# Window attention and a SiLU MLP: products nobody reads, and each pair's work queued one and two pairs later

## The chip, the cores and the metric

The kernel runs on one core of a Trainium2 chip. The core has a matrix engine (TensorE, PE in the profile; its weight loads are PEld), a vector engine (VectorE, DVE), a scalar engine (ScalarE, ACT), GpSimd (POOL), and a queue that issues its transfers (SP). Each engine takes its instructions strictly in the order of its own queue and waits where an input isn't there yet or a buffer isn't free; TensorE's weight loads overlap its products. TensorE writes to PSUM, eight banks of 512 fp32 columns on 128 partitions. The metric is device time in microseconds; lower is better.

## The reference

Eight batches of eight heads, 576 positions, head size 64, all fp32. Attention looks back over 128 positions with a slope on the distance; its output, heads side by side, is the input of an MLP with SiLU:

```python
scores = scale * np.matmul(q, k.transpose(0, 1, 3, 2))
...
mask = (rel >= 0) & (rel < window)          # window = 128
scores = np.where(mask, scores + bias[None], -1000000000.0)
scores = scores - np.max(scores, axis=-1, keepdims=True)
attn = np.exp(scores)
attn = attn / (np.sum(attn, axis=-1, keepdims=True) + 1e-09)
...
h = x @ w_in                                # 4608 x 512 @ 512 x 2048
g = h * (1.0 / (1.0 + np.exp(-h)))
return (g @ w_out).astype(np.float32)       # 4608 x 2048 @ 2048 x 512
```

## The kernel before

The 4608 rows are 36 tiles of 128, made into 9 groups of 512 rows (4 tiles). Attention is done in 72 pairs, two for each tile (a pair is one tile and four of the eight heads). The MLP goes group by group: for each of 16 blocks f of 128 hidden columns, `gemm1` (L379) makes h, `act1` to `act4` make SiLU of it split in a high and a low part, and `gemm2` (L412) adds it to four output tiles. All operands are split in high and low parts, so that three fast products stand for one of full precision. The weights arrive as raw bits and are split on the chip in 32 pieces (`w_split1` on ScalarE, `w_shift` and `w_low` on VectorE, `w_hi` on ScalarE, `w_lo` on VectorE, L448 to L476); four pieces, the list `W_EARLY`, are split ahead of the MLP, the other 28 during its first group.

A pair p goes through these steps; the letters are used from here on. **S(p)** (`scores`, L205): q times k, 16 products (8 in the first tile of a pair of batches, which has no tile behind it). **R(p)** (`row_max`, L229): VectorE adds the slope table and takes the row's maximum, into one of three buffers `t`. **E(p)** (`exps`, L240): ScalarE's exponentials. Then, for the first eight pairs, **T(p)** (`p_transpose_first`, L268), 8 transposes on TensorE into the two PSUM banks "h"; **H(p)** (`p_hi_first`, L278), ScalarE's high part; and **L(p)** (`p_lo_first`, L284), VectorE's low part. **A(p)** (`attend`, L291): 24 small products with v (12 in the first tile), into one of two PSUM banks with the tag "a", of which it uses 260 columns. **N(p)** (`normalize`, L311): VectorE divides by the sum and writes x. Later pairs transpose by DMA instead.

v is scaled by a power of two that comes from its maximum over a pair of batches: nine loads (`vscale_load`, L120), nine reductions (`vscale_reduce`, L127), and three last steps with two small products vt and vs (`vscale_finish`, L141); for the first batches all of that lies at the start of the kernel. GpSimd and VectorE then split v (`v_hi`, `v_lo`, L183 to L199). The scale loads of later batches and the plain v loads share two buffers, "rv".

The order of the work is written out by hand. `put(point, function, ...)` (L481) files a call under a point in time, `at(p)` (L60) gives the point at which pair p begins, and at each point what was filed is issued in the order of filing, each instruction to its engine's queue. Points below zero are the **opening**: pairs 0 to 7, 8 points apart (`STEP`), whose x is then transposed on TensorE (`x_transpose`, L350, PSUM banks "a"), copied to `xh` by ScalarE and `xl` by VectorE. From point 0 on each half of a `gemm1` or `gemm2` is one point, so a group has 64, and the later pairs lie between them. In the opening S(p) stands at n = at(p), R at n+1 and n+2, E at n+2 and n+3, T at n+3 and n+4, H at n+4 and n+5, L at n+11 and n+12, A at n+14, N at n+15 and n+16. So TensorE's queue holds S(p+1), T(p+1), A(p), S(p+2), and so on.

Of the kernel before, what the change touches and what calls it, by code (L numbers as in the profile page):

```python
# [6 lines left out]
F32 = mybir.dt.float32  # L7
F32R = mybir.dt.float32r
F16 = mybir.dt.float16
BF16 = mybir.dt.bfloat16  # L10
# [6 lines left out]
P = 128  # L17
B, H, S, D = 8, 8, 576, 64
NHP = H // 2
DM, DFF = 512, 2048  # L20
# [11 lines left out]
GT = TG // P  # L32
# [17 lines left out]
STEP = 8  # L50
# [3 lines left out]
WD = (1, 1, 2, 3)  # L54

CLOSE = (-4, 2, 8, 14, 20, 26, 32, 38)
W_EARLY = (-18, -15, -9, -6)


def at(p):  # L60

    if p < 2 * GT:
        return STEP * (p - 2 * GT) - 14
    if p < 4 * GT:
        return CLOSE[p - 2 * GT]
    return STEP * (p - 2 * GT) - LEAD
# [3 lines left out]
def tile_window_attention_then_silu_mlp(ctx, tc, qk, v, w_in, w_out, base8, out):  # L70
    nc = tc.nc

    const = ctx.enter_context(tc.tile_pool(name="const", bufs=1))
    pool = ctx.enter_context(tc.tile_pool(name="pool", bufs=2))
    psum = ctx.enter_context(tc.tile_pool(name="psum", bufs=1, space=PSUM))

    ident = const.tile([P, P], F32, name="ident")
    tab = const.tile([P, H, 2 * P], BF16, name="tab")
    ones = const.tile([P, P], F32, name="ones")
    v1 = const.tile([P, VSLOTS, H, D + 1], F16, name="v1")  # L80
    v2 = const.tile([P, VSLOTS, H, D], F16, name="v2")
    weights = {}
# [26 lines left out]
    def next_tag(use):  # L109
        turn[use] = turn.get(use, -1) + 1  # L110
        return bank[use][turn[use] % len(bank[use])]

    def ps_of(tag, name):
        return psum.tile([P, DM], F32, tag=tag, bufs=2 if tag in "ah" else 1, name=name)


    vsc = {}
# [2 lines left out]
    def vscale_load(b, i):  # L120

        tag, bufs = (LAST[XD + i], 1) if b == 0 else ("rv", 2)
        t = pool.tile([P, DM], F32, tag=tag, bufs=bufs, name=f"vm{b}_{i}")
        nc.sync.dma_start(t, v[b, i * P : (i + 1) * P, :])
        vred.setdefault(b, {})[i] = t
# [41 lines left out]
    def block_of(i):  # L167
        return i % NBLK

    def load_k(i):  # L170
        ks[i] = pool.tile([P, NHP, P], F32, tag="k", bufs=KSLOTS, name=f"k{i}")
        nc.sync.dma_start(ks[i], qk[i, 1])

    def load_q(i):
        qs[i] = pool.tile([P, NHP, P], F32, tag="q", bufs=2, name=f"q{i}")
        nc.sync.dma_start(qs[i], qk[i, 0])
# [173 lines left out]
    def x_transpose(cc):  # L350
        xp = ps_of(next_tag("misc"), f"xp{cc}")
        for i in range(GT):
            nc.tensor.transpose(xp[:, i * P : (i + 1) * P], xt[i][:, cc * P : (cc + 1) * P], ident)
        nc.scalar.copy(xh[:, cc], xp)  # L354
        nc.vector.tensor_sub(xl[:, cc], xp, f32(xh[:, cc]))  # L355
# [7 lines left out]
    def x_send():  # L363

        if not w_done():
            return
        for i in [i for i in whole if i // GT <= now[0] + 1]:
            whole.remove(i)
            x_dma(i)

    def x_parts(i):
        t, first = xt[i & -2, "t"][:, i % 2], i % GT * P
        cols, scale = slice(first, first + P), vsc[i // NBLK][:, 1:2]
        nc.scalar.activation(xh[:, :, cols], t[:, :NCC], AF.Copy, scale=scale)  # L374
        nc.gpsimd.tensor_scalar(xl[:, :, cols], t[:, NCC:], scale, 1.0, op0=ALU.mult, op1=ALU.mult)  # L375
# [16 lines left out]
    def act1(n):  # L392
        gt = pool.tile([P, TG], F32, tag="gt", name=f"gt{n}")
        nc.scalar.activation(gt, hps[n], AF.Tanh, scale=0.5 / W_SCALE)  # L394
        gact[n] = gt
# [85 lines left out]
    def put(point, fn, *a):  # L481
        plan.setdefault(max(point, at(0)), []).append((fn, a))

    for p in range(NPAIR):
        i, q = divmod(p, 2)
        n = at(p)
        a = n + (14 if p < 2 * GT else 15 if p < 4 * GT else 13)
        put(n, scores, p)
        if block_of(i) in (SPLIT, SPLIT + 1):
            put(n + 1, other_batch, p)  # L490
        put(n + 1, row_max, p, 0)
        put(n + 2, row_max, p, 1)
        put(n + 2, exps, p, 0)
        put(n + 3, exps, p, 1)
        if p < 2 * GT:
            put(n + 3, p_transpose_first, p, 0)
            put(n + 4, p_hi_first, p, 0)
            put(n + 4, p_transpose_first, p, 1)
            put(n + 5, p_hi_first, p, 1)
            put(n + STEP + 3, p_lo_first, p, 0)  # L500
            put(n + STEP + 4, p_lo_first, p, 1)
        else:
            put(n + 3, p_hi, p, 0)
            put(n + 4, p_lo, p, 0)
            put(n + 4, p_hi, p, 1)
            put(n + 4, p_transpose, p, 0)
            put(n + 5, p_lo, p, 1)
            put(n + 5, p_transpose, p, 1)
        put(a + 0, attend, p)
        put(a + 1, normalize, p, 0)  # L510
        put(a + 2, normalize, p, 1)
        put(a + 3, x_hi, p)
        put(a + 3, x_lo, p)
        if q == 0:
            if i > 1:
                put(at(2 * i - 3) + 1, load_q, i)
                put(at(2 * i - 3) + 1, load_k, i)
            if i >= GT:
                put(n - 2, load_v, i)
            put(a - 3, v_hi, i)  # L520
            put(a - 2, v_lo, i)
    for b in range(1, NBB):
        n = at(2 * NBLK * b)
        for i in range(VCH):
            put(n - 10 * STEP + i * STEP, vscale_load, b, i)
            put(n - 10 * STEP + i * STEP + 6, vscale_reduce, b, i)
        for x in range(3):
            put(n - 6 + 2 * x, vscale_finish, b, x)

# [2 lines left out]
    def later(n, fn, *a):  # L532
        put(pos[0] + n, fn, *a)
# [25 lines left out]
    def begin():  # L559
        for fn, a in plan.pop(pos[0], []):  # L560
            fn(*a)

    with tc.manual_schedule():
        make_identity(nc, ident)
        nc.gpsimd.memset(ones, 1.0)

        warm = const.tile([P, 1], F32, name="warm")
        nc.scalar.activation(warm, ones[:, :1], AF.Exp)
        load_q(0)
        load_k(0)  # L570
        nc.sync.dma_start(tab[:, :, P:], base8[:, :, P:])
        for i in range(VCH):
            vscale_load(0, i)
        load_q(1)
        load_k(1)
        nc.sync.dma_start(tab[:, :, :P], base8[:, :, :P])
        nc.gpsimd.memset(v1[:, :, :, D : D + 1], 1.0)
        for i in range(VCH):
            put(at(0) + 3 + i // 2, vscale_reduce, 0, i)
        for x in range(3):  # L580
            put(at(0) + 8 + x, vscale_finish, 0, x)
        for n in range(2):
            put(at(0) + 14 + 8 * n, w_next_load)
        for n in W_EARLY:
            put(n, w_next)
        for cc, n in enumerate((17, 18)):
            put(at(2 * GT - 2) + n, x_transpose, cc)
        while pos[0] < 0:
            begin()
            pos[0] += 1  # L590
        bank.update(scores=[("a", "a")])

        for g in range(NG):
            now[0] = g

            seq = []
            for f in range(NF):
                n = g * NF + f
                seq += [("g1", n, 0)] + [("xt", 0, 2), ("xt", 0, 3)] * (n == 0) + [("g1", n, 1)]
                if 0 < f < NF - 1:  # L600
                    seq += [("g2", n - 1, 0), ("g2", n - 1, 1)]
            n = g * NF + NF - 1
            for i, x in enumerate([("g2", n - 1, 0), ("g2", n - 1, 1), ("g2", n, 0), ("g2", n, 1)]):
                if g + 1 < NG:
                    seq.append(("xt", g + 1, i))
                seq.append(x)
            for k, n, half in seq:
                if k == "xt":
                    if n == 0:
                        x_transpose(half)  # L610
                    else:
                        x_parts(n * GT + half)
                    continue
                begin()
                x_send()
                if k == "g1":
                    gemm1(n, half)
                    if half == 1:
                        act1(n)
                        later(1, act2, n)  # L620
                        later(2, act3, n)
                        later(2, act4, n)
                else:
                    gemm2(n, half)
                    if n % NF == NF - 1:
                        store(g, 2 * half)
                        store(g, 2 * half + 1)
                if g == 0 and half == 0:
                    w_next()
                pos[0] += 1  # L630
        while plan:
            begin()
            pos[0] += 1
# [35 lines left out]
```

## Time and profile before

| | |
|---|---|
| time, median of 3 runs | 1061.81 us (1060.4 to 1065.43) |
| the profiled execution | 1063.14 us, its span 1061.4 us |
| busy TensorE, VectorE, ScalarE, GpSimd | 996.7, 554.4, 463.4, 248.5 us |
| first S | 4.73 us |
| last S of the opening, S(7) | 55.13 us |
| first product of the MLP | 71.64 us |

The page shows one execution: the busy time of each engine, the span in 40 slices (a digit is the busy share in tenths; PEclk is TensorE's granted clock in tenths of full speed), and the costliest groups of instructions. The timeline gives for each entry start, length, engine, line, operation, what it writes and reads, and in brackets how long the engine stood idle before it and what ended that. A stretch by engine has its length, the busy time of each engine with instructions in brackets, the granted clock, the DMA engines' busy share and GB/s. A busy TensorE is not one at full speed.

### The profile page before, as it was taken

To read this page: it belongs to the slowest core of one execution; us is meant where nothing else is said; L and a number is where in the kernel's file an instruction comes from. 1 tells how busy PE (TensorE), PEld (TensorE's weight loads), DVE (VectorE), ACT (ScalarE), POOL (GpSimd) and SP (SyncE) were. 2 spreads that over 40 slices of the span, in tenths; PEclk is the share of its full clock that TensorE was granted. 3 is DMA by queue.
4 is the path that set the end of the run, shared out by engine and by line. 5 is a ranking of instruction groups with operands and counts; after the bars stand their busy time and mean duration, and the time that the engine had idled before them with its cause. 6 is when DMAs were issued, how large, how long until landed. Compare 5 with 4: busy or idle time off the path is not lost. (4 is left out here: it accounts for less than half of the span.)

```text
span 1061.4 us, 16664 instructions
## 1 busy us (share of the span) xinstructions
PE 996.7 (94%) x6260; PEld 788.0 (74%) x6260; DVE 554.4 (52%) x1358; ACT 463.4 (44%) x968; POOL 248.5 (23%) x228
## 2 busy tenths in 40 slices
PE   4669999999999999999999999999999999999998
PEld 3557777677767776777677777777677777787886
DVE  3568899555546554545455554555455545542111
ACT  4356667534344445434444444433433343333222
POOL 3002222322222222222322222222222222223221
PEclk9968999999999999999999999999899999999999
DMA  6147787623454443433354445433334333331001
GB/s 208 41 138 203 190 234 228 150 60 80 80 126 103 100 100 90 110 70 76 74 110 100 99 100 116 102 69 82 90 80 80 81 100 81 61 48 50 1 1 40
DMA packets 201071, 104.89 MB, mean 99 GB/s; under 512 B 168224, under 2 KB 176416, under 8 KB 200992
## 3 DMA queue, kind: packets, MB, share of 16 engines
q1 hardware_dynamic: 200992, 103.84, 41.4%
q8 instruction: 49, 0.80, 0.3%
q14 instruction: 30, 0.25, 0.1%
HBM read 54.00 MB, written 9.44 MB: 60 GB/s over the span
## 5 line engine op out<-in xcount | busy, mean ns | idle before, releaser
L410 POOL TENSOR_TENSOR gl<-gt,gh 128x512 fp32r<-128x512 f32 x144 | 187.2, 1300 | 749.4 <-ACT gh L405 588.1
L394 ACT ACTIVATE gt<-h 128x512 f32<-128x512 f32 x144 | 86.1, 598 | 453.2 <-PE h L387 445.9
L422 PE MATMUL o<-woh,gh 128*128 128x512 f32 x576 | 232.1, 403 | 12.4 <-ACT gh L405 12.4
L387 PE MATMUL h<-xh,wih 128*128 128x512 f32 x576 | 240.3, 417 | 3.3 <-ACT xh L354 3.3
L399 DVE SCALAR_TENSOR_TENSOR gt<-gt,h 128x512 f32<-128x512 f32 x144 | 98.9, 687 | 266.0 <-ACT gt L394 266.0
L422 PE MATMUL o<-woh,gl 128*128 128x512 f32 x576 | 232.1, 403 | 5.4 <-POOL gl L410 5.3
L422 PE MATMUL o<-wol,gh 128*128 128x512 f32 x576 | 229.3, 398 | 0.0
L387 PE MATMUL h<-xh,wil 128*128 128x512 f32 x576 | 228.3, 396 | 0.0
L387 PE MATMUL h<-xl,wih 128*128 128x512 f32 x576 | 227.9, 396 | 0.0
L258 DVE SCALAR_TENSOR_TENSOR hr<-t,hr 128x512 f16<-128x512 f32 (+1 forms) x128 | 120.6, 942 | 80.0 <-ACT hr L253 79.5
L422 PEld LDWEIGHTS o<-woh,gh 128*128 128x128 f32 x576 | 109.5, 190 | 39.5 <-ACT gh L405 15.5
L422 PEld LDWEIGHTS o<-woh,gl 128*128 128x128 f32 x576 | 109.6, 190 | 36.6 <-POOL gl L410 10.6
L387 PEld LDWEIGHTS h<-xh,wih 128*128 128x128 f32 x576 | 109.4, 190 | 31.5 <-ACT xh L354 3.6
L244 ACT ACTIVATE t<-t,mx 128x256 f32<-128x256 f32 (+1 forms) x288 | 120.5, 486 | 26.8 <-DVE mx L234 26.8
L422 PEld LDWEIGHTS o<-wol,gh 128*128 128x128 f32 x576 | 109.7, 190 | 25.7
L387 PEld LDWEIGHTS h<-xh,wil 128*128 128x128 f32 x576 | 109.1, 189 | 25.5
L387 PEld LDWEIGHTS h<-xl,wih 128*128 128x128 f32 x576 | 109.7, 191 | 20.6 <-DVE xl L355 0.4
L234 DVE CUSTOM_DVE_ANT_0 t<-sp,tab 128x256 f32<-128x256 f32 (+1 forms) x288 | 101.0, 404 | 19.9 <-PE sp L214 13.6
L405 ACT CAST gh<-gt 128x512 fp32r<-128x512 f32 x144 | 88.5, 614 | 48.3 <-DVE gt L399 45.9
L344 DVE TENSOR_TENSOR x<-xs,x 128x256 f16<-128x256 f32 x64 | 73.2, 1143 | 44.7 <-ACT x L338 44.7
L214 PEld LDWEIGHTS sp<-k,q 64*128 64x128 f32 x1088 | 74.2, 205 | 29.6 <-issue 23.8
L214 PE MATMUL sp<-k,q 64*128 64x128 f32 x1088 | 89.2, 306 | 5.3 <-DMA k<-qk 4.7
(62 smaller groups left out, 648.6 us busy)
## 6 DMA issues: line engine op xcount, KB each, us to landing
q<-qk SPq DMA_DIRECT2D x36, 256.0 KB, 3.1
k<-qk SPq DMA_DIRECT2D x36, 256.0 KB, 3.2
vm<-v SPq DMA_DIRECT2D x36, 256.0 KB, 3.6
out<-ot SPq DMA_DIRECT2D x36, 256.0 KB, 2.1
wr<-w_in SPq DMA_DIRECT2D x16, 512.0 KB, 3.9
wr<-w_out SPq DMA_DIRECT2D x16, 512.0 KB, 4.1
rv<-v SPq DMA_DIRECT2D x32, 256.0 KB, 2.9
hl<-hr SPq DMA_TRANSPOSE x128, 3.1
```

The lines of the kernel that those rows point to most:

```text
L214: nc.tensor.matmul(sp[h][:, u, o], qs[i][rows, 2 * q + u], ks[i - 1 + o][rows, 2 * q + u], start=True, stop=True, skip_group_check=True,)
L234: nc.vector.tensor_tensor_reduce(out=t[:, h, 2 * P - n :], in0=st[p]["sp"][h][:, u, o].rearrange("p o c -> p (o c)"), in1=tab[:, 4 * q + 2 ...
L244: nc.scalar.activation(x, x, AF.Exp, bias=st[p]["mx"][:, 2 * u + h : 2 * u + h + 1], scale=-1.0)
L258: nc.vector.scalar_tensor_tensor(out=hr[:, 1], in0=t[:, :, 2 * P - n :], scalar=PSCALE, in1=hr[:, 0], op0=ALU.mult, op1=ALU.subtract)
L344: nc.vector.tensor_sub(xt[i][:, 1, cols], st[p]["x"], xt[i][:, 0, cols])
L387: nc.tensor.matmul(hps[n], w[:, cc], x, start=(half == 0 and i == 0), stop=(half == 1 and i == len(seq) - 1), skip_group_check=True,)
L394: nc.scalar.activation(gt, hps[n], AF.Tanh, scale=0.5 / W_SCALE)
L399: nc.vector.scalar_tensor_tensor(out=gt, in0=gt, scalar=1.0, in1=hps[n], op0=ALU.add, op1=ALU.mult)
L405: nc.scalar.copy(gh, gt)
L410: nc.gpsimd.tensor_sub(gl, gt, f32(gh))
L422: nc.tensor.matmul(ops[ti], a[:, t], w, start=(f == 0 and i == 0), stop=(f == NF - 1 and i == len(seq) - 1), skip_group_check=True,)
```

## The change

For the eight pairs of the opening, T(p) and H(p) move from n+3 .. n+5 to n+9, which is just behind S(p+1) and, on ScalarE, ahead of E(p+1). A(p) moves from n+14 to n+18, behind S(p+2) and T(p+1), and N(p) to n+21 and n+22. L(p) stays at n+11 and n+12. The opening begins 4 points earlier, and the points of the early weight pieces and of the two first `x_transpose` are set anew.

`keep_warm(n)` adds n products of two bf16 tiles full of ones (128 rows, 128 by 252 columns) into columns that A doesn't use of the last allocated bank "a"; nobody reads them. 16 stand ahead of all else, 26 between S(0) and S(1), and for each of the eight pairs 4 behind T(p) and 5 ahead of A(p), 114 in all. They need the tile of ones, for which GpSimd has one more memset; the other memset of ones now comes ahead of the identity.

For the later batches the nine scale loads stand 5 points apart instead of 8, from 54 points ahead of the first use of that scale instead of 80, and each is reduced 4 points after its load instead of 6. For later pairs the expression for N's point is written in another way with the same value.

```diff
-W_EARLY = (-18, -15, -9, -6)
+W_EARLY = (-21, -17, -12, -8)
...
     if p < 2 * GT:
-        return STEP * (p - 2 * GT) - 14
+        return STEP * (p - 2 * GT) - 18
...
+    ones16 = const.tile([P, 2 * P], BF16, name="ones16")
...
+    spare = {}
+
     def ps_of(tag, name):
-        return psum.tile([P, DM], F32, tag=tag, bufs=2 if tag in "ah" else 1, name=name)
+        t = psum.tile([P, DM], F32, tag=tag, bufs=2 if tag in "ah" else 1, name=name)
+        if tag == "a":
+            spare["a"] = t
+        return t
+
+    def keep_warm(n):
+
+        for _ in range(n):
+            nc.tensor.matmul(
+                spare["a"][:, 4 * (D + 1) :], ones16[:, :P], ones16[:, : DM - 4 * (D + 1)],
+                start=True, stop=True, skip_group_check=True,
+            )
...
-        a = n + (14 if p < 2 * GT else 15 if p < 4 * GT else 13)
+        a = n + (2 * STEP + 2 if p < 2 * GT else 15 if p < 4 * GT else 13)
...
         if p < 2 * GT:
-            put(n + 3, p_transpose_first, p, 0)
-            put(n + 4, p_hi_first, p, 0)
-            put(n + 4, p_transpose_first, p, 1)
-            put(n + 5, p_hi_first, p, 1)
+
+            put(n + STEP + 1, p_transpose_first, p, 0)
+            put(n + STEP + 1, p_hi_first, p, 0)
+            put(n + STEP + 1, p_transpose_first, p, 1)
+            put(n + STEP + 1, p_hi_first, p, 1)
             put(n + STEP + 3, p_lo_first, p, 0)
             put(n + STEP + 4, p_lo_first, p, 1)
+
+            put(n + STEP + 1, keep_warm, 4)
+            put(n + 2 * STEP + 2, keep_warm, 5)
...
         put(a + 0, attend, p)
-        put(a + 1, normalize, p, 0)
-        put(a + 2, normalize, p, 1)
-        put(a + 3, x_hi, p)
-        put(a + 3, x_lo, p)
+        z = a + (3 if p < 2 * GT else 1)
+        put(z, normalize, p, 0)
+        put(z + 1, normalize, p, 1)
+        put(z + 2, x_hi, p)
+        put(z + 2, x_lo, p)
...
         for i in range(VCH):
-            put(n - 10 * STEP + i * STEP, vscale_load, b, i)
-            put(n - 10 * STEP + i * STEP + 6, vscale_reduce, b, i)
+            put(n - 54 + 5 * i, vscale_load, b, i)
+            put(n - 50 + 5 * i, vscale_reduce, b, i)
...
     with tc.manual_schedule():
+        nc.gpsimd.memset(ones16, 1.0)
+        nc.gpsimd.memset(ones, 1.0)
         make_identity(nc, ident)
-        nc.gpsimd.memset(ones, 1.0)
+        ps_of("a", "warm")
+        keep_warm(16)
...
+        put(at(0) + 4, keep_warm, 10)
+        put(at(0) + 6, keep_warm, 10)
+        put(at(0) + 7, keep_warm, 6)
         for n in W_EARLY:
             put(n, w_next)
-        for cc, n in enumerate((17, 18)):
+        for cc, n in enumerate((23, 24)):
             put(at(2 * GT - 2) + n, x_transpose, cc)
```

## The prediction

> **What bounds the kernel now.** I read the page's slices first, then the opening (the attention of pairs 0 to 7, ahead of the first MLP product) in the timeline, then busy time by stage. S, R, E, T, H, L, A, N are the steps of a pair as the kernel section names them.
>
> ```profile
> PE   4669999999999999999999999999999999999998
> PEclk9968999999999999999999999999899999999999
> 130.00:150.00 20.00, 18.18 (x120) 14.01 (x118) 19.56 (x43) 14.78 (x32) 6.48 (x4) 1.00 0.84 229
> ```
>
> TensorE (PE) is full in 36 of 40 slices; only the first three, some 80 us, are poor. The third line is a stage of the first token group (columns: length, busy PE, weight loads, VectorE, ScalarE, GpSimd, clock, DMA share, GB/s): VectorE is busy 19.56 of 20 us there, because it splits the weights. So that group is VectorE's, later ones are TensorE's, and neither has an anchor in absolute time: what the opening saves shifts all the rest. This is one step of the opening, from S(4) to S(5):
>
> ```profile
> 33.91 2.08 PE L214 MATMUL sp<-k,q 64*128 64x128 f32 x16
> 36.02 0.42 DVE L234 CUSTOM_DVE_ANT_0 t<-sp,tab 128x256 f32<-128x256 f32 x1 [1.11 <-PE sp L214]
> 36.55 1.71 ACT L244 ACTIVATE t<-t,mx 128x256 f32<-128x256 f32 x4 [3.25 <-DVE mx L234]
> 37.41 1.28 DVE L287 SCALAR_TENSOR_TENSOR hl<-pt,hl 128x512 f16<-128x512 f32 x2
> 38.24 1.94 PE L276 MATMUL pt<-ident,t 128*128 128x128 f32 x8 [2.25 <-DVE hl L287]
> 39.36 0.60 ACT L282 ACTIVATE hl<-pt 128x512 f16<-128x512 f32 x1 [1.10 <-PE pt L276]
> 39.97 1.52 PE L304 MATMUL av<-v,hl 128*128 128x65 f16 x24
> 41.42 2.07 PE L214 MATMUL sp<-k,q 64*128 64x128 f32 x16
> 41.53 0.22 DVE L317 TENSOR_SCALAR r<-av,vsc 128x4 f32<-128x4 f32 x1 [2.84 <-PE av L304]
> 42.00 0.42 DVE L328 TENSOR_TENSOR x<-av,r 128x256 f32<-128x256 f32 x1
> ```
>
> S(4), R(4), E(4), T(4) form a chain, with A(3) queued behind T(4). A step lasts 7.51 us (33.91 to 41.42), and TensorE stands idle for 2.25 of it, until R, L(3) and E are done.
>
> The products are also slow. The same S and A later in the kernel (the chain of waits: start, length, what), and the clock in stretches of 1 us (columns as above):
>
> ```profile
> 874.84 0.74 PE av L304 x24
> 877.07 2.79 PE o L422 x12
> 879.86 1.09 PE sp L214 x16
> ...
> 45.71 0.42 PEld L276 LDWEIGHTS pt<-ident,t 128*128 128x128 f32 x4 [2.51 <-ACT t L244]
> 45.74 1.29 PE L276 MATMUL pt<-ident,t 128*128 128x128 f32 x8 [2.25 <-DVE hl L287]
> ...
> 46.50:47.50 1.00, 1.00 (x16) 0.97 (x16) 0.00 (x0) 0.94 (x2) 0.00 (x0) 0.64 0.08 18
> 49.50:50.50 1.00, 0.83 (x8) 0.56 (x6) 0.13 (x1) 0.00 (x0) 0.00 (x0) 0.66 0.00 0
> 53.50:54.50 1.00, 1.00 (x18) 0.95 (x17) 0.00 (x0) 0.92 (x2) 0.00 (x0) 0.55 0.00 0
> 56.50:57.50 1.00, 0.67 (x8) 0.41 (x4) 0.29 (x1) 0.00 (x0) 0.00 (x0) 0.74 0.00 0
> ```
>
> S takes 2.08 here and 1.09 at 880, A 1.52 and 0.74: the opening runs at half clock. (The clock column's 1.00 before about 46 us is no measurement; S at 33.91 is slow all the same.) If each of the four mixed stretches has one change between 0.5 and 1.0, the changes lie at 46.78 (down), 50.18 (up), 53.6 (down) and 57.02 (up): every 3.4 us a decision. The window 46.78 to 50.18, which A and S fill, is followed by full clock; the next, with an idle 2.25, by half. One window back from this grid, 33.1 to 36.5 was filled to 36.0 (S at 33.91 and an A before it), some 85%, and T at 38.24 was still slow. So a nearly full window is needed, and the present order hardly ever gives one.
>
> **The change, part by part.** *The order.* T(p) and H(p) go behind S(p+1), and A(p) behind S(p+2). In a step k the queues then hold: PE S(k), T(k-1), nine dummies, A(k-2); VectorE R(k), L(k-1), N(k-2); ScalarE H(k-1), E(k). Each wants results from a step earlier. ScalarE has 2 x 0.60 + 1.71 = 2.9 us per step; VectorE R 1.39 (36.02 to 37.41), L 1.28 and N 0.89 (41.53 to 42.42), 3.56 together. Three t buffers suffice: the second half of R(k) waits for half of T(k-1), which is through at 1.6 us into the step, before R's first half ends at 1.8.
>
> *The dummies.* No row shows a bf16 product of 252 columns. At full clock A's product of 65 columns takes 0.74/24 = 31 ns and the MLP's of 512 takes 2.79/12 = 233 ns; the dummy lies between, by columns 252/512 x 233 = 115 ns. Nine cost 0.28 to 2.1, I take 1.03, and at half clock 2.06. They are only a gain through the clock: they fill the windows.
>
> *The step.* T at full clock: weight loads of 0.42 for four, so 0.84 for eight; PE's row of 1.29 has a pause in it; I take 1.0. Step = 1.09 + 1.0 + 1.03 + 0.74 = **3.86 us**, above VectorE's 3.56 and ScalarE's 2.9, and without an idle window. At half clock: 2.08 + 1.73 (38.24 to 39.97) + 2.06 + 1.45 (39.97 to 41.42) = 7.32.
>
> *The start.* All nine v tiles must have come before their scale is known, and A(0) waits for v that GpSimd splits by it:
>
> ```profile
> 15.66 0.56 PE L159 MATMUL vs<-vcol,ones 1*128 1x2 f32 x2 [1.16 <-DVE vcol L156]
> 19.13 0.76 PE L304 MATMUL av<-v,hl 128*128 128x64 f16 x11 [1.10 <-POOL v L194]
> 19.82 2.08 PE L214 MATMUL sp<-k,q 64*128 64x128 f32 x16
> ```
>
> Nothing in the change touches this; the 42 early dummies lie in TensorE's wait for these loads and cost nothing unless they run past vt (some 14.1; at half clock by up to 0.6). S(2) now waits for vs alone, not for A(0): 16.22 instead of 19.82. Half clock: S(2) to 18.30, T(1), four products, to 19.2, nine dummies to 21.2, A(0), twelve products, to 21.9. That is a filled window, so S(3) changes to full clock on its way: with 1.6 + 1.0 + 1.03 + 0.37 S(4) stands at 25.9, and three steps on **S(7) at 37.5**, against 55.13 below. If the clock comes two steps later: 44.4; if the early dummies' clock is kept: 35.5.
>
> *The tail.* From S(7) to the second half of the first MLP product:
>
> ```profile
> 55.13 2.04 PE L214 MATMUL sp<-k,q 64*128 64x128 f32 x16
> 60.58 0.66 ACT L451 ACTIVATE wm<-wr 128x512 f32<-128x512 f32 x1
> 61.27 0.43 DVE L457 TENSOR_SCALAR wm<-wm 128x512 int32<-128x512 int32 x1 [1.40 <-ACT wm L451]
> 61.73 0.69 DVE L462 SCALAR_TENSOR_TENSOR wm<-wr,wm 128x512 int32<-128x512 int32 x1
> 62.46 0.62 ACT L472 CAST wih<-wm 128x512 fp32r<-128x512 f32 x1 [0.73 <-DVE wm L462]
> 63.11 0.69 DVE L476 TENSOR_TENSOR wil<-wm,wih 128x512 fp32r<-128x512 f32 x1 [0.34 <-ACT wih L472]
> 64.19 1.33 PE L353 MATMUL xp<-ident,x 128*128 128x128 f32 x5 [1.45 <-DVE x L328]
> 65.32 0.69 DVE L355 TENSOR_TENSOR xl<-xp,xh 128x512 fp32r<-128x512 f32 x1
> 66.06 0.27 PE L304 MATMUL av<-v,hl 128*128 128x65 f16 x2 [0.55 <-DVE xl L355]
> 69.63 2.08 PE L214 MATMUL sp<-k,q 64*128 64x128 f32 x16
> 71.64 0.79 PE L387 MATMUL h<-xh,wih 128*128 128x512 f32 x1
> 72.53 0.79 DVE L225 MEMSET sp<- 64x384 f32 x2
> 76.82 0.61 ACT L139 ACTIVATE vm<-vm 128x512 f32<-128x512 f32 x1
> 78.59 0.80 PE L387 MATMUL h<-xh,wih 128*128 128x512 f32 x1 [3.31 <-ACT xh L354]
> ```
>
> Before: 23.46 us (55.13 to 78.59). After, counted from S(7): H(6) and E(7) end at 4.65 (1.09 for S, 0.6 for half of T, 1.25 and 1.71); the first weight piece's split, shift, low and hi (now ahead of H(7) in ScalarE's queue) end at 7.15; H(7) 8.4; the second piece's split, shift and low 10.25; L(7), behind them on VectorE, 11.55; its last part and N(6) 13.15; then xp and xh up to xl 14.3 (as 64.19 to 65.32), xl 15.0, third piece's shift and low 16.1, second xl 16.8. The five dummies ahead of A(7) write into the xp tile that this xl reads, so they wait for it, where A(7) waited only for the first xl (66.06): 1.8 us later, and 1.15 for the dummies at half clock, since TensorE idled. A(7) 18.0, S(8) 19.4, first MLP product 21.4. Then the stretch of 6.06 from the MEMSET to 78.59 loses two pieces of work already done or moved (a last part of 0.69, a v tile's |max| of 0.61), leaving 4.8 to 5.2: **26.4**. The tail is thus 2.9 us worse, 0 to 6 at the bounds (no wait of the dummies; one more piece ahead of A(7)).
>
> *The loads of v for the second batch pair's scale* come at 12, 17, ... 52 instead of -14, -6, ... 50: the same nine loads and |max|, two of which left the opening, reduced 4 positions after the load instead of 6. They share two buffers with the other v loads, and SP's queue stands still where neither is free (before and after at point 18, until 21). A position of the first group is some 1.9 us; a load that lands later than 7.6 us would hold up ScalarE. I take 0, bounds -1 and +4. GpSimd's memsets at the start swap places and get one more, all under the wait for the first loads: nothing.
>
> *Sum.* 78.59 - (37.5 + 26.4) = 14.7 us. The profiled run took 1063.14 (span 1061.4), 1.3 above the median of 1061.81: 1048.4 against the former, 1047.1 against the latter, forecast **1048**. Bounds: opening 35.5 to 44.4, tail 23.5 to 29.5, v loads -1 to +4, which rarely add up: 1041 to 1057.
>
> **The rivals.** *Half clock throughout*, the slower one: TensorE's clock unit doesn't take transposes, or products of ones, for work. Then steps cost 7.32: S(4) at 28.5, S(7) at 50.5; S, T and A in the tail add 2.9 to 26.4, 79.8 in all, 1.2 later than now, and the late early dummies 0.5: **1065**, 1070 if the dummies' weight loads aren't hidden. It decides once four of the five steps are slow (4 x 3.46 is what I forecast to gain). For it: no window with transposes in it was full in the trace. Against: windows of A and S were enough, and dummies, A and S make 5.6 us on end. 8%.
>
> Beside it a rule: the Trainium skill ("TensorE: Matmul & The Clock Gate", Part 4: PE-mode transpose) says that transposes don't count as activity in the same way, so that full clock doesn't engage for them. The eight at 45.74 did run at full clock, but whether they earn it no row here shows.
>
> *Clock half of the time*, as transposes counted for nothing would make it: 1.0 of each 3.86 empty, full clock won on dummies, A and S and lost again in some windows. Three steps at (3.86 + 7.32)/2 add 5.2, and the tail 1.5: **1055**. 10%.
>
> *VectorE takes TensorE's place:* if S, R, L and N followed on each other, a step were 1.09 + 1.39 + 1.28 + 0.89 = 4.65, 0.8 more in four steps: **1051**, inside my range; for it speaks 3.56 of 3.86, against it that L and N wait on no S of their step. 10%.
>
> *The opening isn't what starts the MLP:* ScalarE's and VectorE's weight splits, in the tail's order, or the loads of v hold it, and only 2 to 5 us arrive: **1058**. For it: the tail already is their chain. Against: all four pieces are loaded before. 7%.
>
> **How the numbers follow.** The forecast has 65%. A measurement of this kernel tells 0.5% (5.3 us) from no change. Faster (under 1056.5): 65, VectorE's 10, 6 of the clock's 10 and 2 of the last 7, 83%; same: 4 + 4 and 3 of the slow rival's 8, 11%; slower: the other 5 and 1, 6%. The range 1041 to 1058 leaves out the slow rival, part of the last one, and a little on the fast side.
>
> **What would show it.** Right: S(2) near 16.2, S about 1.1 and A 0.75 from S(4) on, steps of 3.7 to 4.1 without idle time on PE, S(7) near 37, the first MLP product near 59 with dummies waiting for xl ahead of A(7), its second half near 64, and from there the old rows 14 to 15 us earlier. Wrong: S at 2.08 up to S(7), steps over 5, a tail beyond 30, or a first group that takes longer than before.

## The result, and the profile after

The changed kernel takes **1046.56 us** (median of 4 runs, 1043.33 to 1047.27), the kernel before 1061.11 (4 runs, 1059.86 to 1065.43): a ratio of 0.985, 95% interval 0.9814 to 0.9885. It is faster by 14.5 us; 1048 was forecast. The profiled executions lie further apart, 1063.14 and 1045.97 us, because the one before lies above its median and the one after below.

The same two page lines after (engine and clock in 40 slices of the span):

```profile
PE   7798898999999999999999999999999999999998
PEclk8899999999999999999999999999899999999999
```

The first three slices read 7, 7, 9 instead of 4, 6, 6; part of what fills them now is the dummies. One step of the opening after, S(5) to S(6), in the timeline:

```profile
27.81 1.16 PE L228 MATMUL sp<-k,q 64*128 64x128 f32 x16
28.90 1.09 PE L290 MATMUL pt<-ident,t 128*128 128x128 f32 x8
29.00 0.42 DVE L248 CUSTOM_DVE_ANT_0 t<-sp,tab 128x256 f32<-128x256 f32 x1 [0.19 <-PE sp L228]
29.83 1.13 PE L125 MATMUL av<-ones 128*128 128x252 bf16 x9
30.40 1.28 DVE L301 SCALAR_TENSOR_TENSOR hl<-pt,hl 128x512 f16<-128x512 f32 x2
30.80 0.89 PE L318 MATMUL av<-v,hl 128*128 128x65 f16 x24
31.61 1.16 PE L228 MATMUL sp<-k,q 64*128 64x128 f32 x16
```

TensorE goes from S to T to the nine dummies to A without a gap, all at full clock, and the step lasts 3.80 us (27.81 to 31.61) instead of 7.51. VectorE, too, stands idle for only 0.19 us ahead of R. How the steps begin, and the tail:

```profile
15.74 2.08 PE L228 MATMUL sp<-k,q 64*128 64x128 f32 x16
18.66 1.60 PE L125 MATMUL vs<-ones 128*128 128x252 bf16 x9
...
35.42 1.16 PE L228 MATMUL sp<-k,q 64*128 64x128 f32 x16
...
47.64 1.33 PE L367 MATMUL xp<-ident,x 128*128 128x128 f32 x5 [5.15 <-DVE x L342]
51.18 1.21 PE L125 MATMUL xp<-ones 128*128 128x252 bf16 x5 [2.21 <-DVE xl L369]
52.18 1.52 PE L318 MATMUL av<-v,hl 128*128 128x65 f16 x24
55.64 0.79 PE L401 MATMUL h<-xh,wih 128*128 128x512 f32 x1
55.86 0.79 DVE L239 MEMSET sp<- 64x384 f32 x2 [0.78 <-PE sp L228]
60.82 0.50 PE L401 MATMUL h<-xh,wih 128*128 128x512 f32 x1 [1.97 <-ACT xh L368]
```

S(2) stands at 15.74 (2.08 us, half clock); the clock changes within the dummies that follow (1.60 us for nine, against 1.13 later), and S(7) stands at 35.42. In the tail TensorE idles 5.15 us until N(6) is through and 2.21 us more with the five dummies waiting for the second xl. The second half of the first MLP product starts at 60.82, 17.8 us earlier than before. The first output, at the end of the first group, is issued 17.7 us earlier (SP's queue; the first row is of the kernel before, the second of the changed one):

```profile
202.43 1.57 SPq L434 DMA_DIRECT2D out<-ot  x2
```

```profile
184.69 1.72 SPq L448 DMA_DIRECT2D out<-ot  x2
```

### The profile page after: what moved, and what is told of

Read it like the earlier page. It is cut to its first block, busy times and chain, and to the rows that moved or that the text cites. A ratio compares the mean times of both kernels' runs of the same rounds, so it can differ in the third digit from the quotient of the medians.

```text
span 1044.2 us, 16900 instructions
## 1 busy us (share of the span) xinstructions
PE 997.2 (95%) x6374; PEld 788.7 (76%) x6374; DVE 555.9 (53%) x1358; ACT 462.3 (44%) x968; POOL 248.5 (24%) x229
## 5 line engine op out<-in xcount | busy, mean ns | idle before, releaser
L228 PEld LDWEIGHTS sp<-k,q 64*128 64x128 f32 x1088 | 68.9, 192 | 25.7 <-issue 25.0
L228 PE MATMUL sp<-k,q 64*128 64x128 f32 x1088 | 83.4, 291 | 1.4 <-DVE xs L342 1.4
```

The source lines that it names most:

```text
L228: nc.tensor.matmul(sp[h][:, u, o], qs[i][rows, 2 * q + u], ks[i - 1 + o][rows, 2 * q + u], start=True, stop=True, skip_group_check=True,)
```

## The experiments

All times are medians of runs beside the kernel before, or single runs where the text says so; three stages are read in the traces: the start of S(7), the start of the second half of the first MLP product ("second half"), and the issue of the first output.

| kernel | S(7) | second half | first output | time |
|---|---|---|---|---|
| before | 55.1 | 78.6 | 202.4 | 1061.1 |
| changed | 35.4 | 60.8 | 184.7 | 1046.6 |
| changed, again | 36.4 | 61.3 | 186.5 | 1045.6 |
| order alone, no dummies | 32.8 | 58.2 | 181.7 | 1043.7 |
| order alone, again | 31.5 | 56.9 | 181.4 | 1042.9 |
| dummies in the old order | 48.1 | 70.7 | 194.4 | 1052.9 |
| without the five dummies of the tail | 36.4 | 60.8 | 184.5 | 1045.7 |
| early dummies as transposes | 35.7 | 60.6 | 185.9 | 1044.3 |
| transposes moved, A not | 42.9 | 67.4 | 193.6 | 1053.0 |
| A moved, transposes not | 43.7 | 67.9 | 191.4 | 1048.9 |
| order alone, v loads as before | 32.6 | 59.1 | 183.5 | 1043.9 |
| order alone, weight pieces later | 31.8 | 55.9 | 181.9 | 1041.1 |
| the same, fourth piece and N(7) moved | 31.4 | 53.5 | 178.0 | 1036.6 |

A caution for the last column: from the first output to the end of the span the thirteen traces take 855.7 to 860.0 us, all of it work that no edit here touches apart from the spacing of v's loads. So up to some 4 us between two times need not come from the opening, and the column of the first output tells more of it.

My theory was that order and clock make the gain together, the dummies earning the clock. The rivals: the dummies make it (by the clock alone), or the order does.

### The order without the dummies

```diff
-        ps_of("a", "warm")
-        keep_warm(16)
...
-        put(at(0) + 4, keep_warm, 10)
-        put(at(0) + 6, keep_warm, 10)
-        put(at(0) + 7, keep_warm, 6)
...
-            put(n + STEP + 1, keep_warm, 4)
-            put(n + 2 * STEP + 2, keep_warm, 5)
```

> The changed kernel without any of the 114 dummies; order and points as changed. Theory A (order and clock both count; without dummies TensorE's step has 1.09 + 1.0 + 0.74 = 2.8 us of work at full clock against VectorE's 3.56): steps run dense at half clock until a full window grants full clock, then VectorE sets the step at 3.6 to 3.8 with 0.8 us of idle TensorE, and the clock may fall back now and then. S(7) at 35 to 38, and the tail about 3 us shorter because A(7) doesn't wait behind the five dummies: second half of the first MLP product at 57 to 61, time 1043 to 1048. Theory B (the dummies carry the gain): full clock is rarely granted, steps of 5.3 us (2.08 + 1.73 + 1.45), S(7) at 42 or later, second half of the first MLP product beyond 65, time 1050 to 1056.

1043.74 us (4 runs, 1041.86 to 1044.95), ratio to before 0.9811 (0.9772 to 0.9851); a second time, on another chip, 1042.85 (5 runs, 1041.01 to 1045.04). TensorE in the timeline of the first:

```profile
15.99 2.08 PE L228 MATMUL sp<-k,q 64*128 64x128 f32 x16
18.00 1.11 PE L290 MATMUL pt<-ident,t 128*128 128x128 f32 x4
18.91 0.87 PE L318 MATMUL av<-v,hl 128*128 128x65 f16 x12
19.70 2.08 PE L228 MATMUL sp<-k,q 64*128 64x128 f32 x16
...
23.27 1.16 PE L228 MATMUL sp<-k,q 64*128 64x128 f32 x16
...
29.46 1.16 PE L228 MATMUL sp<-k,q 64*128 64x128 f32 x16
30.96 1.22 PE L290 MATMUL pt<-ident,t 128*128 128x128 f32 x8 [0.34 <-DVE hl L301]
32.02 0.89 PE L318 MATMUL av<-v,hl 128*128 128x65 f16 x24
32.84 1.16 PE L228 MATMUL sp<-k,q 64*128 64x128 f32 x16
```

Theory B falls. The order alone fills the windows: at half clock S, T, A, S follow each other without a gap from 15.99 on, and S(4) at 23.27 is fast. From S(6) on T waits 0.34 us for L, and VectorE sets the step: R(5) starts at 28.75 and R(6) at 32.13, 3.38 us later, with no idle time of VectorE between. That is shorter than the 3.80 that TensorE needs with the dummies in it. So the dummies have nothing to do in the dense order and cost 0.4 us a step: S(7) stands 2.6 us later with them. One part of the expectation missed: the tail isn't 3 us shorter, but 25.3 us (32.84 to 58.17) against 25.4 with the dummies.

### The dummies in the old order

```diff
+        keep_warm(16)
...
+            put(n + 2, keep_warm, 9)
             put(n + 3, p_transpose_first, p, 0)
```

> The kernel before, its order and points untouched, with 16 dummies ahead of S(0) and 9 between S(p) and T(p) of each pair of the opening, where TensorE waits 2.25 us. Theory A: half clock makes a full window at once, full clock follows and holds, the idle 2.25 us stays because R, E and L aren't TensorE's: steps of 1.1 + 2.25 + 1.1 + 0.74 = 5.2 us instead of 6.9 to 7.5, S(7) at 44 to 47 instead of 55.1, the second half of the first MLP product at 68 to 71, some 9 us gained. Theory C (the order is the whole gain): full clock is lost again in each step to the idle time that is left, steps stay near 7, S(7) at 52 to 56, the time that of before within 3 us.

1052.88 us (one run), 8 to 9 below before. A step in the timeline (from S to S 5.28 us, 27.00 to 32.28):

```profile
28.09 1.14 PE L125 MATMUL av<-ones 128*128 128x252 bf16 x9
30.41 1.22 PE L290 MATMUL pt<-ident,t 128*128 128x128 f32 x8 [1.18 <-DVE hl L301]
32.28 1.16 PE L228 MATMUL sp<-k,q 64*128 64x128 f32 x16
```

Full clock comes at the first full window and holds, although 1.18 us of each 5.28 stay idle; steps and time are as theory A had them. S(7) at 48.1 is later than expected, as S(2) came at 20.89: nine dummies stood between vt and vs. So the two parts don't add: about 8 to 9 us by the dummies alone (one run), about 18 by the order alone, 14.5 with both; at the first output 8.0, 20.7 and 17.7.

### Without the five dummies ahead of A(7)

```diff
-            put(n + 2 * STEP + 2, keep_warm, 5)
+            if p < 2 * GT - 1:
+                put(n + 2 * STEP + 2, keep_warm, 5)
```

> The changed kernel without the five dummies ahead of A(7) alone. My tail: they wait for the second xl and cost 2.9 us between them (1.8 of wait, 1.15 of work at half clock), so A(7) and S(8) come 2.5 to 3 us earlier, the second half of the first MLP product 2 to 3 us earlier than 60.8, and the time falls by 2 to 3 us against the changed kernel. Rival: VectorE's queue (third and fourth weight piece ahead of N(7) and R(8)) sets that point anyway, and nothing is gained.

1045.72 us (4 runs, 1044.43 to 1048.48), no difference from the changed kernel that can be told. From S(7) the first product comes 17.5 us later instead of 20.2, as expected, but the second half 24.4 instead of 25.4 (24.9 in the changed kernel's second trace):

```profile
50.53 1.47 PE L318 MATMUL av<-v,hl 128*128 128x65 f16 x24 [0.55 <-DVE xl L369]
...
54.67 0.69 DVE L490 TENSOR_TENSOR wol<-wm,woh 128x512 fp32r<-128x512 f32 x1 [0.34 <-ACT woh L486]
55.28 0.42 DVE L342 TENSOR_TENSOR x<-av,r 128x256 f32<-128x256 f32 x1
55.85 0.79 DVE L239 MEMSET sp<- 64x384 f32 x2 [0.15 <-issue]
```

A(7) starts 1.65 us earlier in the trace, yet the MEMSET ahead of R(8) stands at 55.85 against 55.86: it is VectorE's queue, with the fourth weight piece and N(7) in it, that holds R(8), E(8) and, behind them on ScalarE, the next xh. The rival was right.

### Early dummies as transposes

```diff
-        keep_warm(16)
+        turn_ident(16)
...
+    def turn_ident(n):
+        for _ in range(n):
+            nc.tensor.transpose(spare["a"][:, 3 * P :], ident, ident)
```

The 26 between S(0) and S(1) are replaced in the same way.

> The changed kernel with the 42 early dummies (16 ahead of S(0), 26 between S(0) and S(1)) made into transposes of the identity tile, 128 by 128 in fp32; the 72 later ones as they were. If transposes count as activity: full clock by S(1), 8 products in 0.71 us as in the changed kernel, and S(2) at 15.7. If they don't: S(1) takes 1.23 us, as in the kernel before. The time is within 2 us of the changed kernel's in both cases, since the loads of v set S(2).

```profile
1.75 3.67 PE L133 MATMUL warm<-ident 128*128 128x128 f32 x16 [1.75 <-POOL ident masks.py:199]
5.36 1.23 PE L232 MATMUL sp<-k,q 64*128 64x128 f32 x8
6.51 3.22 PE L133 MATMUL warm<-ident 128*128 128x128 f32 x26
9.66 0.71 PE L232 MATMUL sp<-k,q 64*128 64x128 f32 x8
```

S(0) takes 1.23 us, S(1), behind 26 transposes, 0.71; in the kernel before, where no such filling stands ahead of it, S(1) takes 1.23. S(0) alone would fill 1.15 us (5.36 to 6.51) of a window of 3.4, so the fp32 transposes earn full clock here, against the rule of the Trainium skill ("TensorE: Matmul & The Clock Gate", Part 4: PE-mode transpose). (The trace lists them as MATMUL and doesn't show in which mode they ran.) That takes the ground from the two rivals that rested on it. The time, 1044.3 (one run), is the changed kernel's.

### Half of the order

T and H moved, A and N in their old place (first edit), and the other way round (second), both without dummies:

```diff
-        a = n + (2 * STEP + 2 if p < 2 * GT else ...)
+        a = n + (14 if p < 2 * GT else ...)
...
-        z = a + (3 if p < 2 * GT else 1)
+        z = a + 1
```

> No dummies; T(p) and H(p) behind S(p+1) as changed, but A(p) at its old n+14, ahead of S(p+2), so that it waits for L(p) of its own step. Theory A: TensorE waits in each step for R, H and L, 2.75 us from the end of S to A at full clock: steps of 4.6 us if full clock comes, 6.7 if it stays at half; S(7) at 41 to 50 against 32.8 with the whole order. Rival: moving the transposes is what counts and A's place doesn't: S(7) at 35 or less.

```diff
-            put(n + STEP + 1, p_transpose_first, p, 0)
-            put(n + STEP + 1, p_hi_first, p, 0)
...
+            put(n + 3, p_transpose_first, p, 0)
+            put(n + 4, p_hi_first, p, 0)
...
```

> No dummies; A(p) and N(p) behind S(p+2) as changed, but T(p) and H(p) in their old place, ahead of S(p+1). Theory A: T(k) still waits in its own step for R(k), E(k) and L(k-1), 2.25 us with no other work, so the windows stay unfilled: steps of 7 to 7.5 at half clock (5.3 at best), only S(2) comes 3.6 us earlier because A(0) no longer stands ahead of it: S(7) at 48 to 52, time 1056 to 1059. Rival: A's place is what counts: S(7) at 40 or less.

A step of each in the timeline, transposes moved first:

```profile
38.56 1.16 PE L228 MATMUL sp<-k,q 64*128 64x128 f32 x16
39.65 1.09 PE L290 MATMUL pt<-ident,t 128*128 128x128 f32 x8
41.00 0.23 PE L318 MATMUL av<-v,hl 128*128 128x65 f16 x2 [0.25 <-ACT hl L296]
41.89 1.07 PE L318 MATMUL av<-v,hl 128*128 128x65 f16 x22 [0.66 <-DVE hl L301]
42.90 1.16 PE L228 MATMUL sp<-k,q 64*128 64x128 f32 x16
```

```profile
39.11 1.16 PE L228 MATMUL sp<-k,q 64*128 64x128 f32 x16
40.21 0.90 PE L318 MATMUL av<-v,hl 128*128 128x65 f16 x24
42.52 1.22 PE L290 MATMUL pt<-ident,t 128*128 128x128 f32 x8 [1.42 <-DVE hl L301]
43.67 1.16 PE L228 MATMUL sp<-k,q 64*128 64x128 f32 x16
```

1052.99 and 1048.87 us (one run each). In the first, A waits for the H and L of its own step, 4.34 us a step, as expected. In the second my expectation missed: T waits 1.42 us a step for L, but A now lies under that wait and full clock did come, from S(5) at 34.55 on; steps of 4.56 us. (S(7) stands at nearly the same place in both; of the 4 us between the times 2.2 are there at the first output.) Each half takes a part of the waiting away; together they leave 0.34 us of it, and the step at VectorE's 3.4 us.

### The v loads

```diff
-            put(n - 54 + 5 * i, vscale_load, b, i)
-            put(n - 50 + 5 * i, vscale_reduce, b, i)
+            put(n - 10 * STEP + i * STEP, vscale_load, b, i)
+            put(n - 10 * STEP + i * STEP + 6, vscale_reduce, b, i)
```

> The order alone (no dummies), with the nine loads for the later v scales back at their old points, 8 apart from -80 on, each reduced 6 points after. I priced their move at 0, bounds -1 and +4 (positive: the new spacing costs). As priced: within 1 us of the order alone, 1043 to 1045. If the loads in the opening and early in the first group stand in ScalarE's way (two |max| of 0.8 us lie in the tail's chain): 1 to 2 us slower than the order alone. If the new spacing blocks the first group: 1 to 4 us faster.

1043.94 us (6 runs, 1039.34 to 1048.0) against 1043.74 and 1042.85 of the order alone: no difference that these runs could tell. The tail is 1.2 us longer than in the first run of the order alone (26.5 against 25.3 from S(7) to the second half), which agrees with the |max| work that lies in it again.

### The tail

> The changed kernel itself, once more beside the others on one chip: 1043 to 1048, 14 to 16 us below the kernel before.

1045.55 us (6 runs, 1045.17 to 1050.05). Beside it, on the same chip, the order alone with the weight pieces later:

```diff
-W_EARLY = (-21, -17, -12, -8)
+W_EARLY = (-15, -12, -9, -6)
```

> The order alone (no dummies), with the four early weight pieces at points -15, -12, -9 and -6 instead of -21, -17, -12 and -8, so that H(7), L(7) and N(6) come ahead of most of them in ScalarE's and VectorE's queues. Theory A (the tail from S(7), 25.3 us to the second half of the first MLP product with the order alone, is a ping-pong of ScalarE and VectorE over the pieces, with L(7) and N(6) queued behind it): the tail shortens to 21 to 23.5 us, S(7) unchanged near 33, the time falls by 2 to 4 us below the order alone, to 1040 to 1042. Rival: the pieces are wanted by the first products as early as they are, and what the tail gains comes back as waits in the first group: within 1 us of the order alone.

1041.08 us (6 runs, 1040.27 to 1043.6), ratio to before 0.9784 (0.9744 to 0.9824). The tail falls to 24.1 us only, and the first output leaves no earlier than with the order alone (181.9 against 181.7): what the tail gained comes back in the first group, as the rival had it. So the lower time is not shown to come from the opening. S(8) now starts at 43.68 instead of 49.32, but VectorE's queue still has the fourth piece ahead of N(7) and R(8):

```profile
50.38 0.98 PE L367 MATMUL xp<-ident,x 128*128 128x128 f32 x5 [3.63 <-DVE x L342]
51.62 0.91 ACT L258 ACTIVATE t<-t,mx 128x256 f32<-128x256 f32 x2 [0.98 <-DVE mx L248]
55.32 1.04 ACT L368 CAST xh<-xp 128x512 fp32r<-128x512 f32 x2
```

The transposes of x that the second half needs wait for N(7), and E(8) for R(8). The wait of E(8) is the one that counts: xh stands behind E(8) in ScalarE's queue and comes at 55.32, long after the transposes. So that piece and N(7) were moved as well:

```diff
-W_EARLY = (-15, -12, -9, -6)
+W_EARLY = (-15, -12, -9, -2)
...
-        z = a + (3 if p < 2 * GT else 1)
+        z = a + (3 if p < 2 * GT - 1 else 1)
```

> The order alone with three early weight pieces at -15, -12, -9, the fourth at -2, and N(7) right behind A(7) instead of two points later. In the run with the pieces at -15 to -6 the second x transposes waited 3.63 us for N(7), which stood behind the fourth piece. Theory A (this tail is a chain of queues): the second half of the first MLP product at 51 to 54 instead of 55.9. But VectorE's work isn't less, and it sets the first group: the first output leaves at 180 to 182 as with the pieces at their changed points (181.7), and the time stays within 1.5 us of the order alone. Rival: the 2 to 4 us arrive: first output before 179.5, time below 1040.

**1036.6 us** (5 runs, 1035.54 to 1041.84), ratio 0.9777 (0.9752 to 0.9802), against 1042.85 of the order alone beside it:

> The order alone once more, on the chip of the next one: 1042 to 1045.

```profile
47.41 1.04 PE L367 MATMUL xp<-ident,x 128*128 128x128 f32 x8
53.52 0.80 PE L401 MATMUL h<-xh,wih 128*128 128x512 f32 x1 [5.07 <-ACT xh L368]
```

The second transposes of x wait no more; the product still waits for xh, which stands behind E(8) in ScalarE's queue. The second half starts 3.4 us earlier than in the order alone beside it, and the first output leaves 3.4 us earlier too (178.0 against 181.4). Here the rival was right: what the tail saves arrives. The medians lie 6.3 us apart; the traces show 3.4 of that ahead of the first output and another 3.4 behind it (856.3 against 859.7 us to the end of the span), and the cause of the latter stays open. It is the fastest of these kernels, and has none of the dummies.

## Why the prediction was right, and where it was not

- **What bounds the kernel** held. From the second half on, the first group takes 123.8 us before (78.6 to 202.4) and 123.9 after (60.8 to 184.7): the opening's gain is passed on whole. Over all thirteen traces it is 123.5 to 126.2, so some 2.5 us can be lost there.
- **The step** held: 3.86 forecast, 3.80 measured; T, A and S at full clock as read from later rows. A dummy costs 0.97/9 = 108 ns (29.83 to 30.80), 115 taken. VectorE's 3.56 us a step as the next bound showed in the order alone: 3.38.
- **The start** was sized a little high: S(7) at 37.5, measured 35.4 and 36.4. I let the clock change in S(3); in the profiled run it changed in the dummies before it.
- **The tail** held as an order of waits (the dummies for the second xl, then A(7), S(8)), 26.4 forecast, 25.4 and 24.9 measured. But its cost of 2.9 us for these dummies was put on the wrong stage: they delay the first product by 2.7 us, counted from S(7), the second half, from which the rest follows, by 1.0 or less, because VectorE's queue holds back the MEMSET to the same time (55.85 against 55.86) without them.
- **The step that failed** is the dummies': "They are only a gain through the clock: they fill the windows". In the old order they do; in the new one nothing is left to fill. At half clock S, T and A are dense without them, which my own sum showed (2.08 + 1.73 + 1.45, all on one engine, more than VectorE's 3.56): I priced the kernel with the dummies and never without. They cost about 3 us: 2.8 between the first medians and 2.7 between the second ones (no pair side by side on one chip, and the first pair's ranges overlap), and 3 to 5 at the first output, which all four traces agree on.
- **The rivals.** Half clock throughout, and half of the time: neither occurred, and the transposes earn the clock. VectorE in TensorE's place: not with the dummies, but in the order alone, at 3.38 rather than 4.65 us, since R, L and N don't follow on their own step. The opening not being what starts the MLP: wrong, though the tail, ScalarE's and VectorE's chain, is where the last experiment found 3.4 us at the first output.
- **The sum** was 3 us short where it was made, at the second half of the profiled pair: 14.7 forecast, 17.8 measured, 2.1 of the difference from S(7) and 1.0 from the tail. It is right for the medians (14.5), and that closeness is in part luck: the median of the kernel before alone lay between 1061.1 and 1065.3 from one set of runs to the next.

## What to carry to other kernels

When the engines' queues are in order, a chain of small steps is paid in full for each item unless the next item's independent work stands ahead of the waiting instruction; moving the transposes one item and the products with v two items back took 7.5 us steps to 3.4, and each half of the move alone to about 4.5 (full clock, which each of the three orders earned by itself, is part of that). Filling a clock window with products that nobody reads helped here only while the order left holes: make the order dense first, then measure whether any are needed. Behind a dense stage look at the hand-over: here weight pieces in two engines' queues stood ahead of short steps that the next stage waited for.

## What the runs showed of the hardware

TensorE's clock is decided about every 3.4 us: in the trace before it changes at 46.78, 50.18, 53.60 and 57.02. It takes more to earn full clock than to keep it. Counted back from these changes, a window filled to 84% (2.87 of 3.41 us, 33.12 to 36.53) didn't earn it, as T at 38.24 was still slow, and filled ones did, while a window with 2.25 us idle (34% busy) lost it. With the dummies in the old order it was kept through 1.18 idle us in each 5.28. Two further traces give windows between. In the order alone the clock falls at 42.58 (the stretch 42.40 to 42.80 has 0.73); with A moved and the transposes not, it falls at some 28.9 (28.80 to 29.00 has 0.72). Ahead of its first fall the column reads 1.00 in any case, but T at 37.70 in the former (1.23 us for eight) and at 27.85 in the latter (1.28) ran at full speed. The two windows ahead of the first fall, then the one ahead of the second and the one behind it (length, busy PE, weight loads, VectorE, ScalarE, GpSimd, clock, DMA share, GB/s):

```profile
35.78:39.18 3.40, 1.97 (x39) 1.68 (x36) 3.33 (x14) 2.56 (x6) 0.00 (x0) 1.00 0.32 121
39.18:42.58 3.40, 0.84 (x19) 0.60 (x15) 1.84 (x4) 2.15 (x4) 0.00 (x0) 1.00 0.35 113
...
25.50:28.91 3.41, 1.63 (x22) 1.26 (x20) 3.20 (x13) 2.09 (x5) 0.00 (x0) 1.00 0.46 154
28.91:32.32 3.41, 3.41 (x42) 3.03 (x40) 1.34 (x8) 1.42 (x4) 0.00 (x0) 0.50 0.02 5
```

The window that was 58% busy kept full clock, those with 25% and 48% lost it. Where between 58% and 48% the line runs, these windows don't tell. And fp32 transposes count for it, as the run with the early transposes shows.
